# Attention pairs in one run of scores and one of values, small products in one place: a routed attention and mixer kernel on Trainium2

## The chip, the cores and the metric

The kernel runs on one core of one Trainium2 chip. A core has engines that work side by side, each through its own stream of instructions in order: TensorE (matrix products, called PE in the profile, with its weight loads under PEld), VectorE (DVE), ScalarE (ACT), GpSimd (POOL) and SyncE (SP), which issues transfers here. They wait for each other through semaphores. Matrix products are written to PSUM, a memory of eight banks; everything else lies in SBUF. The metric is the device time of the whole kernel in microseconds (us).

## What is computed

A routed attention with 4 batches and 8 heads, 768 tokens and head size 64, and after it an MLP mixer over tokens and channels:

```python
q_assign = argmax(einsum('bhsd,hcd->bhsc', q_n, c_n), axis=-1)     # 16 centroids per head
k_assign = argmax(einsum('bhsd,hcd->bhsc', k_n, c_n), axis=-1)
mask = q_assign[:, :, :, None] == k_assign[:, :, None, :]
scores = scale * matmul(q, k.transpose(0, 1, 3, 2))
scores = where(mask, scores, -1e9)
attn = softmax(scores)
attn_out = matmul(attn, v)
x = attn_out as (B, S, H * D)
h = maximum(x^T @ w_tok1, 0) @ w_tok2
u = x + h^T
out = u + maximum(u @ w_ch1, 0) @ w_ch2
```

(q_n, k_n and c_n are normalised rows. All arrays are fp32.)

## The kernel before

The attention goes over 16 pairs of heads (4 batches times 4 pairs). In a pair, two heads of 64 rows share TensorE, so its matmuls use parts of the 128 x 128 array. A pair's queries are two halves of 384 (`qh`), its keys six tiles of 128 (`j`). The scores and the mask are products into one PSUM tile of two banks; ScalarE takes the exponential into SBUF; VectorE adds the six exponentials of a half up; TensorE multiplies them with the values.

PSUM before: one bank `ps_w`, one bank `ps_av`, and three tiles of two banks `ps_sc`. The pools of SBUF that matter:

```python
    ps_w = pool("ps_w", 1, space=PSUM)
    ps_av = pool("ps_av", 1, space=PSUM)
    ps_sc = pool("ps_sc", 3, ps_sc_stack, space=PSUM)
    ...
    loads = pool("loads", 3, attention)      # values of a pair
    work = pool("work", 6, attention)        # exponentials
    sums = pool("sums", 2, attention)
    qkpool = pool("qkpool", 2, routing, side="right")
```

The products of a pair:

```python
    def scores(g, qh):
        ...
        for j in range(NJ):
            ...
            sc = ps_sc.tile([P, 2, 512], F32, tag="sc", name="sc")
            for src, start in ((st["ohT"], True), (st["T"], False)):
                for h in range(2):
                    rows = slice(h * D, (h + 1) * D)
                    nc.tensor.matmul(
                        sc[:, h, 0:HS], lhsT=src[rows, 1, j], rhs=src[rows, 0, js],
                        start=start, stop=not start,
                    )
            ex = st["ex", j] = work.tile([P, 2, HS], F32, name="ex")
            nc.scalar.activation(out=ex, in_=sc[:, :, 0:HS], func=ACT.Exp, scale=SM_SCALE)

    def add_up(g, qh):
        ...
        for j in range(1, NJ):
            nc.vector.tensor_tensor(
                out=acc, in0=acc if j > 1 else st["ex", 0], in1=st["ex", j], op=ALU.add
            )

    def values(g, qh):
        av = ps_av.tile([P, HS], F32, name="av")
        for j in range(NJ):
            ex = st.pop(("ex", j))
            for h in range(2):
                nc.tensor.matmul(
                    av[h * D : (h + 1) * D], lhsT=st["va"][:, h, j], rhs=ex[:, h],
                    start=(j == 0), stop=(j == NJ - 1),
                )
        ...
        nc.scalar.copy(out=st["avT"][:, js].rearrange("p j t -> p (j t)"), in_=av)
```

Beside these, each pair needs small products. `pair_sums` adds the sums up over the partitions (four column strips of 32, 384 wide), `route_products` multiplies the rows of a coming pair with the centroids (the same shape), `half_turn` transposes a half of the attention's result on TensorE (three transposes). What they give is taken by VectorE: `pair_denominators` and `pair_reciprocals`, `route` (a transpose, a maximum, two comparisons into one-hots), and `half_out`, which scales the result into the mixer's input. `turn` transposes the 32 x 32 blocks of a coming pair's queries and keys on VectorE, two instructions of 128 x 768. `route_turn` transposes one-hots through the DMA; `route_count` is a small sum on ScalarE.

The weights of the mixer are rounded during the attention. The work stands in 21 steps. One step does the VectorE and GpSimd part of piece i-2 (three VectorE instructions and one GpSimd add), the ScalarE part of piece i-1 (two instructions), and the load of piece i.

The loop before:

```python
    for g in range(NPAIR):
        more, old, final = g < NPAIR - 1, g - 1, g == NPAIR - 1
        if g + 2 < NPAIR:
            load(g + 2)
        ...
        scores(g, 0)
        if g == 0:
            turn(1)
        add_up(g, 0)
        rounding(1)
        values(g, 0)
        if more or old >= 0:
            two = ps_sc.tile([P, 2, 512], F32, tag="sc", name="small")
            if old >= 0:
                pair_sums(old, two[:, 0, 0:HS])
            if more:
                route_products(g + 1, two[:, 1, 0:HS])
            if old >= 0:
                pair_denominators(old)
            if more:
                route(g + 1)
                route_big(g + 1)
                route_turn(g + 1)
            if old >= 0:
                pair_reciprocals(old)

        scores(g, 1)
        if more:
            route_count(g + 1)
        add_up(g, 1)
        if g + 2 < NPAIR:
            turn(g + 2)
        values(g, 1)
        if old >= 0:
            two = ps_sc.tile([P, 2, 512], F32, tag="sc", name="px")
            for qh in range(2):
                half_turn(old, qh, two[:, qh, 0:HS])
            for qh in range(2):
                half_out(old, qh)
        rounding(g < EARLY or final)        # EARLY = 6
```

After the loop come the sums of the last pair in `ps_w`, then the mixer (token products `tok1` and `tok2`, then channel products), whose matmuls use the whole array.

Of the kernel before, what the change touches and what calls it, by code (L numbers as in the profile page):

```python
# [17 lines left out]
C = 16  # L18
P = 128
# [11 lines left out]
QP = P // NQ  # L31
NPAIR = B * NF

EARLY = 6
SM_SCALE = 0.125


# [8 lines left out]
def kernel(  # L46
# [37 lines left out]
            tc.tile_pool(name=name, bufs=bufs, reuse_waits="tile", **kw)  # L84
        )

    ps_w = pool("ps_w", 1, space=PSUM)
    ps_av = pool("ps_av", 1, space=PSUM)
    ps_sc_stack = fast.enter_context(ExitStack())
    ps_sc = pool("ps_sc", 3, ps_sc_stack, space=PSUM)  # L90

# [38 lines left out]
    def load(g):  # L130


        b, f = divmod(g, NF)
        st = state.setdefault(g, {})
        st["qk"] = qkpool.tile([P, 2, NJ, NQ, QP], F32, name="qk")
        st["va"] = loads.tile([P, 2, NJ, D], F32, name="va")
        for a, src in ((1, k), (0, q)):
            for c in range(NQ):
                h, d0 = 2 * f + c // 2, (c % 2) * QP
                nc.sync.dma_start(  # L140
                    st["qk"][c * QP : (c + 1) * QP, a].rearrange("r j i d -> r (j i) d"),
                    src[b, h, :, d0 : d0 + QP].rearrange("(i r j) d -> r j i d", i=NQ, j=NJ),
                )
        nc.sync.dma_start(
            st["va"], v[b, 2 * f : 2 * f + 2].rearrange("h (p j) d -> p h j d", p=P)
        )
# [91 lines left out]
    def centroids_norm(cen):  # L238
        sq = rsmall.tile([P, D], F32, name="censq")
        ss = rsmall.tile([P, 1], F32, name="ss")  # L240
        nc.vector.tensor_tensor(out=sq, in0=cen, in1=cen, op=ALU.mult)
        nc.vector.reduce_sum(out=ss, in_=sq, axis=AX.X)
        lo = rsmall.tile([P, 1], F32, name="lo")
        nc.vector.tensor_scalar_max(out=lo, in0=ss, scalar1=float(2.0**-100))


        nrm = rsmall.tile([P, 1], F32, name="nrm0")
        nc.vector.tensor_scalar(
            out=nrm.bitcast(I32), in0=lo.bitcast(I32), scalar1=0.5, scalar2=float(0x1FBB6875),
            op0=ALU.mult, op1=ALU.add,  # L250
        )
# [18 lines left out]
        pc = ps_w.tile([P, H * C], F32, tag="w", name="pc")  # L270
        nc.tensor.transpose(out=pc, in_=cn.rearrange("p i d -> p (i d)"), identity=ident)
        return pc

# [72 lines left out]


    def load_first():
        st = state[0] = {"qk": qkpool.tile([P, 2, NJ, NQ, QP], F32, name="qk")}
        st["va"] = loads.tile([P, 2, NJ, D], F32, name="va")  # L350
        st["T"] = qktp.tile([P, 2, NJ, P], F32, name="qkT")
        st["ohT"] = qktp.tile([P, 2, NJ, P], BF16, name="ohT")
        st["rows"] = st.pop("qk").rearrange("p a j i d -> p (a j i d)").rearrange(
            "p (n a j h d) -> p n a j h d", n=2, a=2, h=2, j=HJ
        )
        for n in range(2):
            for a, src, queue in ((1, k, nc.sync), (0, q, nc.scalar)):
                for h in range(2):
                    queue.dma_start(
                        st["rows"][:, n, a, :, h],  # L360
                        src[0, h].rearrange("(p j) d -> p j d", p=P)[:, HJ * n : HJ * n + HJ],
                    )
        nc.sync.dma_start(st["va"], v[0, 0:2].rearrange("h (p j) d -> p h j d", p=P))

    def turn_first(n, tiles):

        st = state[0]
        js = slice(HJ * n, HJ * n + HJ)
        for a in (1, 0):
            for j in range(HJ):  # L370
                nc.tensor.transpose(
                    out=tiles[a][:, j * P : (j + 1) * P],
                    in_=st["rows"][:, n, a, j].rearrange("p h d -> p (h d)"), identity=ident,
                )
        return [(st["T"][:, a, js].rearrange("p j t -> p (j t)"), tiles[a]) for a in range(2)]

    def route_turn_first(n):
        po = ps_w.tile([P, 2, HJ, P], BF16, tag="w", name="po")
# [27 lines left out]
    def scores(g, qh):  # L406
        st = state[g]
        js = slice(HJ * qh, HJ * qh + HJ)
        for j in range(NJ):
# [3 lines left out]
            for src, start in ((st["ohT"], True), (st["T"], False)):  # L413
                for h in range(2):
# [6 lines left out]
            nc.scalar.activation(out=ex, in_=sc[:, :, 0:HS], func=ACT.Exp, scale=SM_SCALE)  # L421

    def add_up(g, qh):
        st = state[g]
        if qh == 0:
            st["sum"] = sums.tile([P, 2, 2, HS], F32, name="sum")
        acc = st["sum"][:, qh]
        for j in range(1, NJ):
            nc.vector.tensor_tensor(  # L429
                out=acc, in0=acc if j > 1 else st["ex", 0], in1=st["ex", j], op=ALU.add  # L430
            )

    def values(g, qh):
        st = state[g]
        av = ps_av.tile([P, HS], F32, name="av")
        for j in range(NJ):
            ex = st.pop(("ex", j))
            for h in range(2):
                nc.tensor.matmul(  # L439
                    av[h * D : (h + 1) * D], lhsT=st["va"][:, h, j], rhs=ex[:, h],  # L440
# [285 lines left out]
            nc.vector.tensor_reduce(out=good[:, i : i + 1], in_=ok, axis=AX.X, op=ALU.min)  # L726

    def fits_count():
        pn = ps_w.tile([1, 3], F32, tag="w", name="pn")
# [11 lines left out]
    def begin():  # L741
# [11 lines left out]
        for oh in ohs:  # L753
            nc.gpsimd.memset(oh, 0.0)
        load(1)
        pw = ps_av.tile([P, HS], F32, name="av")

        def keep_warm(n):
            for _ in range(n):
# [29 lines left out]
    for b in range(B):  # L789
        if b + 1 < B:  # L790
            ends += [lambda b=b, t=t: tok1(b + 1, t) for t in range(NT)]
        ends += [lambda b=b, j=j: tok2(b, j) for j in range(NJ)]

    def rounding(n):
        for _ in range(min(n, len(weights))):
            weights.pop(0)()

    for g in range(NPAIR):
        more, old, final = g < NPAIR - 1, g - 1, g == NPAIR - 1
        if g + 2 < NPAIR:  # L800
            load(g + 2)
        if final:
            assert not weights
            routing.close()
            W["ch2"] = pool("wc2pool", 1, side="right").tile([P, NCT, DM], F32, name="wc2")
            weights = list(weight_steps(stage, W, ("ch2",)))

        scores(g, 0)
        if g == 0:
            turn(1)  # L810
        add_up(g, 0)
        rounding(1)
        values(g, 0)
        if more or old >= 0:
            two = ps_sc.tile([P, 2, 512], F32, tag="sc", name="small")
            if old >= 0:
                pair_sums(old, two[:, 0, 0:HS])
            if more:
                route_products(g + 1, two[:, 1, 0:HS])
            if old >= 0:  # L820
                pair_denominators(old)
            if more:
                route(g + 1)
                route_big(g + 1)
                route_turn(g + 1)
            if old >= 0:
                pair_reciprocals(old)

        scores(g, 1)
        if more:  # L830
            route_count(g + 1)
        add_up(g, 1)
        if g + 2 < NPAIR:
            turn(g + 2)
        values(g, 1)
        if old >= 0:
            two = ps_sc.tile([P, 2, 512], F32, tag="sc", name="px")
            for qh in range(2):
                half_turn(old, qh, two[:, qh, 0:HS])
            for qh in range(2):  # L840
                half_out(old, qh)
        rounding(g < EARLY or final)

    pair_sums(NPAIR - 1, ps_w.tile([P, HS], F32, tag="w", name="den"))
    pair_denominators(NPAIR - 1)
    pair_reciprocals(NPAIR - 1)
    ps_sc_stack.close()
    pools["ps_m"] = pool("ps_m", 2, space=PSUM)
    for m in range(9):
        ends.pop(0)()  # L850
        if m == 0:
            half_turn(NPAIR - 1, 0, ps_w.tile([P, HS], F32, tag="w", name="px"))
            half_turn(NPAIR - 1, 1, ps_av.tile([P, HS], F32, name="av"))
            for qh in range(2):
                half_out(NPAIR - 1, qh)
        if m % 3 == 2:
# [243 lines left out]
```

## Time and profile before

| | |
|---|---|
| time, median of 3 | 877.78 us (877.59 to 877.98) |
| span of the profiled execution | 875.5 us |
| TensorE busy | 862.4 us, 4294 matmuls |
| VectorE busy | 504.9 us |
| ScalarE busy | 297.8 us |
| GpSimd busy | 44.2 us |
| granted TensorE clock | 0.998 |

The attention takes the first 333 us of the span, the mixer the rest. A line of the profile's groups gives the source line, the engine and the operation, then what it writes and reads with shapes. For a matmul the shape begins with the part of the array that it uses, rows * columns: 64*128 is one of two row halves, 128*64 one of two column halves, 128*32 one of four strips. An fp32 product stands as two matmuls. A matmul's recorded length covers its way through the array, and neighbours overlap, so what one costs in a stream is read from the distance of starts and not from its length. In a timeline, neighbours of one kind are merged; the first number is the start, the second how long the merged run lasts, and a bracket tells the idle time before it and who ended it.

### The profile page before, as it was taken

Reading aid. Unit: us, or ns where it says so; the run is one execution under the profiler, and the core shown is the slowest. Engines: PE = TensorE matmul, PEld = TensorE weight load, DVE = VectorE, ACT = ScalarE, POOL = GpSimd, SP = SyncE. Lnnn points to the kernel's source line nnn. Section 1 sums busy time; section 2 is a strip of 40 time slices with the busy share of each in tenths; the row PEclk is TensorE's granted clock in tenths of the full one; section 3 lists DMA queues with packets and bytes.
Section 4 is the critical chain, followed back from the end, with each engine's and each line's share of the span. In section 5 each row is a group of like instructions: output and inputs, shape, how many; then the busy total and the mean of one; then the engine's idle time right before and its main releaser. Section 6 shows DMA issues by size and latency. Waiting matters only on the chain.

```text
span 875.5 us, 11022 instructions
## 1 busy us (share of the span) xinstructions
PE 862.4 (99%) x4294; PEld 522.8 (60%) x4294; DVE 504.9 (58%) x848; ACT 297.8 (34%) x506; POOL 44.2 (5%) x40
## 2 busy tenths in 40 slices
PE   9999999999999999999999999999999999999996
PEld 4444444444444444444578686685876867768675
DVE  6798898888878862895553433423344333443332
ACT  4666566666556551321210211203112031130210
POOL 1010011000010000330000000000000000000000
PEclk9999999999999999999999999999999999999999
DMA  8665675544443130420000010000010000100001
GB/s 153 156 123 119 140 139 115 126 109 97 97 97 73 20 90 0 144 72 1 0 1 1 0 37 37 0 1 0 36 38 1 0 1 25 48 1 1 0 25 51
DMA packets 133275, 47.61 MB, mean 54 GB/s; under 512 B 122080, under 2 KB 126176, under 8 KB 133216
## 3 DMA queue, kind: packets, MB, share of 16 engines
q1 hardware_dynamic: 131616, 46.45, 23.0%
q8 instruction: 35, 0.57, 0.3%
q10 hardware_dynamic: 1600, 0.39, 0.2%
q14 instruction: 24, 0.20, 0.1%
HBM read 34.64 MB, written 6.29 MB: 47 GB/s over the span
## 4 chain that ended last, share of the span: by engine, by line
PE 95%; DVE 3%; ACT 1%; issue 0%; DVEq 0%
PE sc L416 18%; PE av L439 15%; PE pX L690 14%; PE pX L639 14%; PE pZ L690 7%; PE pZ L639 7%; PE ph L508 4%; PE pY L690 4%; PE pY L639 4%; PE pu L517 3%; PE px L468 1%; PE small L455 1%; PE pt L580 1%; PE small L296 1%; DVE wh L209 1%; DVE wT L214 1%
## 5 line engine op out<-in xcount | busy, mean ns | idle before, releaser
L421 ACT ACTIVATE ex<-sc 128x768 f32<-128x768 f32 x192 | 152.6, 811 | 44.8 <-PE sc L416 42.6
L416 PE MATMUL sc<-qkT 64*128 64x384 f32 x768 | 155.1, 482 | 0.0
L429 DVE TENSOR_TENSOR sum<-sum,ex 128x768 f32<-128x768 f32 x128 | 125.3, 979 | 13.7 <-ACT ex L421 0.5
L439 PE MATMUL av<-ex,va 128*64 128x384 f32 x768 | 130.9, 490 | 0.0
L439 PEld LDWEIGHTS av<-ex,va 128*64 128x64 f32 x768 | 52.2, 137 | 74.8 <-issue 71.0
L416 PEld LDWEIGHTS sc<-qkT 64*128 64x128 f32 x768 | 68.2, 188 | 34.8 <-issue 34.6
L639 PE MATMUL pX<-uT,wc 128*128 128x384 f32 x192 | 67.4, 487 | 0.0
L416 PE MATMUL sc<-ohT 64*128 64x384 bf16 x384 | 63.0, 324 | 0.3 <-DVE ohT L389 0.2
L647 ACT COPY p<-pX 128x384 f32<-128x384 f32 x24 | 11.4, 475 | 148.1 <-PE pX L639 148.1
L639 PEld LDWEIGHTS pX<-uT,wc 128*128 128x128 f32 x192 | 36.2, 190 | 24.7 <-issue 1.0
L221 POOL TENSOR_TENSOR wc<-wT,wup 128x512 int32<-128x512 int32 x24 | 32.0, 1334 | 253.5 <-ACT avT L446 132.0
L429 DVE TENSOR_TENSOR sum<-ex 128x768 f32<-128x768 f32 x32 | 32.0, 1001 | 20.3 <-ACT ex L421 20.2
L446 ACT COPY avT<-av 128x384 f32<-128x384 f32 x32 | 15.3, 479 | 83.1 <-PE av L439 83.1
L508 PE MATMUL ph<-x,wt 128*128 128x512 f32 x96 | 42.0, 594 | 1.2 <-DVE x L520 0.7
L517 PE MATMUL pu<-h,wt 128*128 128x512 f32 x96 | 42.0, 592 | 0.0
L534 DVE TENSOR_TENSOR c<-pZ,u 128x384 f32<-128x384 f32 x24 | 13.4, 557 | 46.9 <-PE pZ L639 46.9
L416 PEld LDWEIGHTS <-ohT 64*128 64x128 bf16 x384 | 19.2, 94 | 35.4 <-issue 13.6
L534 DVE TENSOR_TENSOR x<-pX,x 128x256 f32<-128x256 f32 x24 | 10.2, 423 | 49.3 <-PE pX L690 49.3
L534 DVE TENSOR_TENSOR hA<-pY,p 128x384 f32<-128x384 f32 x24 | 13.4, 557 | 40.4 <-PE pY L639 40.4
L690 PE MATMUL pX<-w2s,hA 128*128 128x256 f32 x144 | 35.1, 380 | 0.5 <-DVE x L534 0.5
L690 PE MATMUL pX<-wc,hA 128*128 128x256 f32 x144 | 35.0, 379 | 0.0
L690 PE MATMUL pZ<-w2s,hS 128*128 128x256 f32 x144 | 35.0, 379 | 0.0
(129 smaller groups left out, 1196.5 us busy)
## 6 DMA issues: line engine op xcount, KB each, us to landing
raw<-in_moe_w_ch_dram SPq DMA_DIRECT2D x24, 512.0 KB, 4.3
qk<-in_k_dram SPq DMA_DIRECT2D x64, 96.0 KB, 4.0
va<-in_v_dram SPq DMA_DIRECT2D x16, 384.0 KB, 4.0
out_dram<-x SPq DMA_DIRECT2D x24, 256.0 KB, 2.0
qk<-in_q_dram SPq DMA_DIRECT2D x60, 96.0 KB, 3.4
raw<-in_moe_w_tok_dram SPq DMA_DIRECT2D x3, 512.0 KB, 4.6
raw<-in_moe_w_tok_dram SPq DMA_DIRECT2D x4, 384.0 KB, 4.0
qk<-in_q_dram ACTq DMA_DIRECT2D x4, 96.0 KB, 3.1
```

The costliest lines, as they stand in the source:

```text
L221: nc.gpsimd.tensor_tensor(out=dst.bitcast(I32), in0=T, in1=up, op=ALU.add)
L416: nc.tensor.matmul(sc[:, h, 0:HS], lhsT=src[rows, 1, j], rhs=src[rows, 0, js], start=start, stop=not start,)
L421: nc.scalar.activation(out=ex, in_=sc[:, :, 0:HS], func=ACT.Exp, scale=SM_SCALE)
L429: nc.vector.tensor_tensor(out=acc, in0=acc if j > 1 else st["ex", 0], in1=st["ex", j], op=ALU.add)
L439: nc.tensor.matmul(av[h * D : (h + 1) * D], lhsT=st["va"][:, h, j], rhs=ex[:, h], start=(j == 0), stop=(j == NJ - 1),)
L446: nc.scalar.copy(out=st["avT"][:, js].rearrange("p j t -> p (j t)"), in_=av)
L508: nc.tensor.matmul(pf, lhsT=W["tok1"][:, j, t * P : (t + 1) * P], rhs=xs[b][:, j], start=(j == 0), stop=(j == NJ - 1),)
L517: nc.tensor.matmul(pu, lhsT=W["tok2"][:, t, j], rhs=h1s[b][:, t], start=(t == 0), stop=(t == NT - 1))
L534: nc.vector.tensor_tensor(out=dst, in0=a, in1=b, op=ALU.add)
L639: nc.tensor.matmul(psum, lhsT=A[a][:, k, c * P : (c + 1) * P], rhs=R[r][:, k], start=start and k == 0, stop=k == 1, skip_group_check=not s ...
L647: nc.scalar.copy(out=kept[name], in_=psum)
L690: nc.tensor.matmul(psum, lhsT=h2[a][:, k, i * P : (i + 1) * P], rhs=Bw[w][:, 3 * part + k], start=start and k == 0, stop=k == 2, skip_grou ...
```

## The change

A pair is treated as one unit. Both halves' scores come first, all 12 blocks, then both halves' values. The small products come at one place per pair: the transposes of the pair before, then the sums of this pair and the route products of the pair after next in one PSUM tile. So the routing runs two pairs ahead instead of one. For 12 blocks of exponentials there are nine buffers, and the three score tiles in PSUM hold the rest. `ps_w` goes, and `ps_av` has two banks, so that the second half's values needn't wait for the copy of the first. A rounding step stands between scores and values in each pair, and six of the pairs have a second one at their end; before, the first six pairs had a second one after the values. Loads of values are issued on their own, and the rows of the first pair are loaded into two of the exponential buffers.

The aim of the order is that TensorE stays longer with one kind of product. The diff, with small renamings cut (`...`):

```diff
-EARLY = 6
+EARLY = 13
+
+EX = 9
...
-    ps_w = pool("ps_w", 1, space=PSUM)
-    ps_av = pool("ps_av", 1, space=PSUM)
+    ps_av = pool("ps_av", 2, space=PSUM)
...
-    loads = pool("loads", 3, attention)
+    loads = pool("loads", 2, attention)
...
-    work = pool("work", 6, attention)
+    work = pool("work", EX, attention)
...
-            ex = st["ex", j] = work.tile([P, 2, HS], F32, name="ex")
+            ex = st["ex", qh, j] = work.tile([P, 2, HS], F32, name="ex")
...
-            st["sum"] = sums.tile([P, 2, 2, HS], F32, name="sum")
+            st["sum"] = sums.tile([P, 2, 2, HS], F32, name="sum", bufs=1)
...
+    load_v(1)
     for g in range(NPAIR):
-        more, old, final = g < NPAIR - 1, g - 1, g == NPAIR - 1
-        if g + 2 < NPAIR:
-            load(g + 2)
+        final = g == NPAIR - 1
...
-        (the loop's body as shown above)
+        for qh in range(2):
+            scores(g, qh)
+            if g == 0 and qh == 0:
+                turn(1)
+                load(2)
+            if (g, qh) == (0, 1):
+                route_products(1, ps_av.tile([P, HS], F32, tag="av", name="pr"))
+                route_on(1)
+            add_up(g, qh)
+        for other in (1, 2) if g == 1 else (g + 1,) if 2 <= g < NPAIR - 1 else ():
+            route_count(other)
         if g + 2 < NPAIR:
             turn(g + 2)
+        if g + 3 < NPAIR:
+            load(g + 3)
+        rounding(1)
+        for qh in range(2):
+            values(g, qh)
+        if g + 2 < NPAIR:
+            load_v(g + 2)
+
+        if g > 0:
             two = ps_sc.tile([P, 2, 512], F32, tag="sc", name="px")
             for qh in range(2):
+                half_turn(g - 1, qh, two[:, qh, 0:HS])
+        two = ps_sc.tile([P, 2, 512], F32, tag="sc", name="small")
+        pair_sums(g, two[:, 0, 0:HS])
+        if g + 2 < NPAIR:
+            route_products(g + 2, two[:, 1, 0:HS])
+        if g > 0:
+            for qh in range(2):
+                half_out(g - 1, qh)
+        pair_denominators(g)
+        if g + 2 < NPAIR:
+            route_on(g + 2)
+        pair_reciprocals(g)
+        rounding(final or g % 2 == 0 and 0 < g < EARLY)
+
-    pair_sums(NPAIR - 1, ps_w.tile([P, HS], F32, tag="w", name="den"))
-    pair_denominators(NPAIR - 1)
-    pair_reciprocals(NPAIR - 1)
...
```

(`route_on` is `route`, `route_big` and `route_turn` in one.)

More of the change, by code (lines that the diff above doesn't have):

```diff
@@ L135, in load @@
         st["qk"] = qkpool.tile([P, 2, NJ, NQ, QP], F32, name="qk")
-        st["va"] = loads.tile([P, 2, NJ, D], F32, name="va")
         for a, src in ((1, k), (0, q)):
@@ L143, in load, with load_v @@
                 )
+    def load_v(g):
+        b, f = divmod(g, NF)
+        st = state[g]
+        st["va"] = loads.tile([P, 2, NJ, D], F32, name="va")
         nc.sync.dma_start(
@@ L269, in centroids_norm @@
         )
-        pc = ps_w.tile([P, H * C], F32, tag="w", name="pc")
+        pc = ps_av.tile([P, H * C], F32, tag="av", name="pc")
         nc.tensor.transpose(out=pc, in_=cn.rearrange("p i d -> p (i d)"), identity=ident)
@@ L348, in load_first @@
     def load_first():
-        st = state[0] = {"qk": qkpool.tile([P, 2, NJ, NQ, QP], F32, name="qk")}
-        st["va"] = loads.tile([P, 2, NJ, D], F32, name="va")
+        st = state[0] = {}
         st["T"] = qktp.tile([P, 2, NJ, P], F32, name="qkT")
         st["ohT"] = qktp.tile([P, 2, NJ, P], BF16, name="ohT")
-        st["rows"] = st.pop("qk").rearrange("p a j i d -> p (a j i d)").rearrange(
-            "p (n a j h d) -> p n a j h d", n=2, a=2, h=2, j=HJ
-        )
+        st["rows"] = [
+            work.tile([P, 2, HS], F32, name="ex").rearrange("p a (j h d) -> p a j h d", h=2, d=D)
+            for _ in range(2)
+        ]
         for n in range(2):
@@ L359, in load_first @@
                     queue.dma_start(
-                        st["rows"][:, n, a, :, h],
+                        st["rows"][n][:, a, :, h],
                         src[0, h].rearrange("(p j) d -> p j d", p=P)[:, HJ * n : HJ * n + HJ],
                     )
-        nc.sync.dma_start(st["va"], v[0, 0:2].rearrange("h (p j) d -> p h j d", p=P))
     def turn_first(n, tiles):
@@ L372, in turn_first @@
                     out=tiles[a][:, j * P : (j + 1) * P],
-                    in_=st["rows"][:, n, a, j].rearrange("p h d -> p (h d)"), identity=ident,
+                    in_=st["rows"][n][:, a, j].rearrange("p h d -> p (h d)"), identity=ident,
                 )
@@ L377, in route_turn_first @@
     def route_turn_first(n):
-        po = ps_w.tile([P, 2, HJ, P], BF16, tag="w", name="po")
+        po = ps_av.tile([P, 2, HJ, P], BF16, tag="av", name="po")
         for a in (1, 0):
@@ L429, in add_up @@
             nc.vector.tensor_tensor(
-                out=acc, in0=acc if j > 1 else st["ex", 0], in1=st["ex", j], op=ALU.add
+                out=acc, in0=acc if j > 1 else st["ex", qh, 0], in1=st["ex", qh, j], op=ALU.add
             )
@@ L434, in values @@
         st = state[g]
-        av = ps_av.tile([P, HS], F32, name="av")
+        av = ps_av.tile([P, HS], F32, tag="av", name="av")
         for j in range(NJ):
-            ex = st.pop(("ex", j))
+            ex = st.pop(("ex", qh, j))
             for h in range(2):
@@ L728, in fits_count @@
     def fits_count():
-        pn = ps_w.tile([1, 3], F32, tag="w", name="pn")
+        pn = ps_av.tile([1, 3], F32, tag="av", name="pn")
         nc.tensor.matmul(pn, lhsT=ones[:, 0:1], rhs=good, start=True, stop=True)
@@ L755, in begin @@
         load(1)
-        pw = ps_av.tile([P, HS], F32, name="av")
+        load_v(0)
+        pw = ps_av.tile([P, HS], F32, tag="av", name="av")
         def keep_warm(n):
@@ L792, with route_on @@
         ends += [lambda b=b, j=j: tok2(b, j) for j in range(NJ)]
+    def route_on(g):
+        route(g)
+        route_big(g)
+        route_turn(g)
     def rounding(n):
@@ L806 @@
             weights = list(weight_steps(stage, W, ("ch2",)))
[L808 to L832, printed above, removed]
+        for qh in range(2):
[9 more added lines that the diff above has]
+            route_count(other)
@@ L833 @@
         if g + 2 < NPAIR:
             turn(g + 2)
-        values(g, 1)
-        if old >= 0:
+        if g + 3 < NPAIR:
[6 more added lines that the diff above has]
+        if g > 0:
             two = ps_sc.tile([P, 2, 512], F32, tag="sc", name="px")
             for qh in range(2):
-                half_turn(old, qh, two[:, qh, 0:HS])
-            for qh in range(2):
-                half_out(old, qh)
@@ L842 @@
-        rounding(g < EARLY or final)
-    pair_sums(NPAIR - 1, ps_w.tile([P, HS], F32, tag="w", name="den"))
-    pair_denominators(NPAIR - 1)
-    pair_reciprocals(NPAIR - 1)
+                half_turn(g - 1, qh, two[:, qh, 0:HS])
[4 more added lines that the diff above has]
+        if g > 0:
+            for qh in range(2):
+                half_out(g - 1, qh)
@@ L851 @@
         if m == 0:
-            half_turn(NPAIR - 1, 0, ps_w.tile([P, HS], F32, tag="w", name="px"))
-            half_turn(NPAIR - 1, 1, ps_av.tile([P, HS], F32, name="av"))
+            half_turn(NPAIR - 1, 0, ps_av.tile([P, HS], F32, tag="av", name="px"))
+            half_turn(NPAIR - 1, 1, ps_av.tile([P, HS], F32, tag="av", name="av"))
             for qh in range(2):
```

## The prediction

> **What bounds the kernel now.** I read the busy table first, then the chain, then TensorE's timeline over one pair of heads, then the other engines over the same stretch. The first two, from the page of the kernel before:
>
> ```profile
> PE 862.4 (99%) x4294; PEld 522.8 (60%) x4294; DVE 504.9 (58%) x848; ACT 297.8 (34%) x506; POOL 44.2 (5%) x40
> ...
> PE 95%; DVE 3%; ACT 1%; issue 0%; DVEq 0%
> ```
>
> TensorE never rests. No other engine's wait can be shortened to any use; the time falls only if TensorE does less, or does the same with fewer losses between matmuls. The waits of TensorE that the trace names come to about 7 us in the whole run, with none in the 15 full pairs. So I looked at one pair on TensorE, instruction by instruction (columns: start, length, instruction; lines of the score loop left out):
>
> ```profile
> 251.71 0.34 PE L416 MATMUL sc<-ohT 64*128 64x384 bf16 x2
> ...
> 255.76 0.33 PE L416 MATMUL sc<-ohT 64*128 64x384 bf16 x2
> 255.92 0.81 PE L416 MATMUL sc<-qkT 64*128 64x384 f32 x4
> 256.66 4.09 PE L439 MATMUL av<-ex,va 128*64 128x384 f32 x24
> 260.68 0.85 PE L455 MATMUL small<-sum,ones 128*32 128x384 f32 x8
> 261.35 0.83 PE L296 MATMUL small<-qkT,cnd 128*32 128x384 f32 x8
> 262.11 0.34 PE L416 MATMUL sc<-ohT 64*128 64x384 bf16 x2
> ...
> 271.08 0.88 PE L468 MATMUL px<-ident,avT 128*128 128x128 f32 x6
> 271.89 0.34 PE L416 MATMUL sc<-ohT 64*128 64x384 bf16 x2
> ```
>
> The pair takes 271.89 - 251.71 = 20.18 us. In it TensorE changes its tile shape six times: 64*128 (scores) to 128*64 (values) to 128*32 (small) to 64*128 to 128*64 to 128*128 (px) to 64*128. Within one shape the starts in the trace are evenly spaced: a score block of one key tile 0.807, a step of two value matmuls 0.3225, a step of four small ones 0.322, a px transpose 0.109. At a change of shape the last step is longer, in every one of the 15 pairs alike: 0.416 after scores, 0.422 after values, 0.439 after small (by starts of the step's first matmul; 0.322 each without a change), 0.205 after px for 0.109. The first step of the new shape is a little longer too: 0.374 for the first value step, 0.346 for small, 0.169 for px, and 0.011 more for scores. Together a change costs:
>
> - scores to values 0.094 + 0.051 = 0.145
> - values to small 0.100 + 0.023 = 0.123; values to px 0.100 + 0.060 = 0.160
> - small to scores 0.117 + 0.011 = 0.128; px to scores 0.096 + 0.011 = 0.107
>
> Check: work without changes is 12 x 0.807 + 24 x 0.3225 + 4 x 0.322 + 6 x 0.109 = 19.37; changes 0.145 x 2 + 0.123 + 0.128 + 0.160 + 0.107 = 0.81; sum 20.18, as measured. In the mixer part after the pairs, where all is 128*128, going from one kind of product to another shows no such step (0.429 before and at the border). The loss belongs to the shape.
>
> **What the Trainium skill says.** "TensorEngine Tiling (Array Packing)", Tiling Modes, Key Properties: "Changing tiling mode (not just tile) drains the TensorE". The trace agrees, about 0.10 us a time. "TensorE: Matmul & The Clock Gate", Part 2, Step-by-step, says that between matmuls of a stream the drain of one overlaps the fill of the next; agreed, a pair of 384-column bf16 matmuls is 0.162 apart from what follows. "GPSIMD Engine Reference", 1. Specifications, says GpSimd shares SBUF interfaces with VectorE and contends with an instruction that has two SBUF inputs. The adds are such: four take 4.15 us alone, 5.03 beside a rounding add of GpSimd.
>
> **The change, part by part.**
>
> *Order on TensorE.* The pair becomes 12 score blocks, 12 value blocks, px of the pair before, then sums and route products as one run of 128*32. Four changes of shape: scores to values 0.145, values to px 0.160, px to small, small to scores 0.128. Px to small is seen once before, at the end of the attention (px at 330.97, sums at 331.78: 0.81, as px to scores): 0.096 + 0.023 = 0.12. Sum 0.55 for 0.81: **0.255 us less per pair**, period 19.92. The count of matmuls is the same. Fifteen pairs: 3.8 us.
>
> *Last pair.* Its sums come with the other small ones and no longer as a group of their own: the same count of changes is saved, already counted in the 3.8; I add 0.1 for the extra change that the old end had.
>
> *First pair.* Sums of pair 0 and products for pair 2 now stand at its end. The products need pair 2's transposed rows, and VectorE turns those after adding up pair 0. Scores begin at 10.14, go on to about 20.5, products for pair 1 to 21.3, values to 29.3, sums to 30.0. VectorE: route of pair 1 from 21.4 (2.1 us), five adds 5.15 to 28.7, turn 1.8 to 30.5. So TensorE waits there about 0.5 us, once.
>
> *Exponentials: nine buffers and three score tiles in PSUM for 12 blocks.* Blocks 10 to 12 are computed into PSUM, but their exponentials wait until the first value blocks give buffers back. Times from the first score matmul of a pair: values start at 9.8, the first block is through at 10.6, exponential 10 runs to 11.5, 11 and 12 follow at 0.72 (the spacing that ScalarE showed when it was behind) to 12.9. TensorE needs exponential 10 only in the tenth value block, at 9.8 + 9 x 0.645 = 15.6. No wait.
>
> *VectorE.* A pair's busy time is 16.3 us with one rounding step and 18.6 with two; both under 19.9. But the order counts now:
>
> ```profile
> 254.45 0.96 DVE L429 TENSOR_TENSOR sum<-ex 128x768 f32<-128x768 f32 x1 [1.61 <-ACT ex L421]
> 255.51 4.15 DVE L429 TENSOR_TENSOR sum<-sum,ex 128x768 f32<-128x768 f32 x4
> 259.58 0.42 DVE L204 TENSOR_SCALAR wh<-wh 128x512 f32<-128x512 f32 x1
> ...
> 262.24 0.58 DVE L459 STREAM_TRANSPOSE dent<-small 128x384 f32<-128x384 f32 x1 [0.99 <-PE small L296]
> ...
> 264.85 0.96 DVE L429 TENSOR_TENSOR sum<-ex 128x768 f32<-128x768 f32 x1
> ```
>
> From these: adds begin 2.74 after the pair (254.45 - 251.71), five take 5.13, rounding 1.6, the block from denominators to reciprocals 2.6. In the new order: seven adds to 9.95, three more behind the late exponentials 11.6 to 14.7, turn to 16.4, rounding to 18.0. The last px transpose starts at 18.3 and half_out can follow 0.3 later (as 271.68 to 271.99 before): 18.6 to 19.6, denominators and the route transpose to 20.7, the rest to 22.2. TensorE wants px's tile back for the second score block at 20.7 and the small tile for the third at 21.5: 1.1 and 0.8 us of slack. The next adds start at 19.92 + 2.74 = 22.7, after 22.2. With a second rounding step, at the end of six pairs, VectorE reaches the next adds 1.15 late and loses 0.9 to GpSimd, most of which its wait for exponential 10 takes up: the add that would start at 11.6 starts at about 12. Still in time for half_out.
>
> *Buffers and loads.* Rows, values and one-hots are asked for about a pair ahead of use or more; a load takes 4 us. Off the path. The larger exponential pool replaces the third load buffer and the second sum buffer; the sum tile is read at 18.5 and written again 4 us later.
>
> Sum: 15 x 0.255 + 0.1 (end) + 0.1 (one change fewer in pair 0) - 0.5 (wait in pair 0) = 3.5 us. 877.8 - 3.5 = **874.2**.
>
> **Rivals.**
> 1. *The exponentials become a gate.* If a buffer came back only when the whole first half of the values is done, exponential 10 would start near 13.9: adds to 18, turn to 20, route products (wanted at 19.1) late by over 1, half_out with rounding near 22.5, the second score block late by 2. Some 2 to 2.5 us a pair, 30 to 38 us in all, near 910. Against it: today a reader's release is seen one matmul group after it (exponential 1 starts at 252.74, 0.53 after its last score matmul starts), and the buffer's readers are two value matmul pairs.
> 2. *VectorE's order bites in the pairs with two roundings.* My slack there is under 1 us. If it is used up in six to twelve pairs by 0.3 to 0.5 us, 2 to 5 us are lost: 876 to 879. For it: adds of up to 1.84 us beside GpSimd in the trace. Against it: the step that collided with the adds is at most once per place now.
> 3. *The drain isn't saved.* If px to small cost much more than the single sight at 331.78 says, or the border between the two score halves or the two value halves cost something, 0.1 to 0.2 a pair goes: 876.
>
> **Range and chances.** All terms are under half a per cent. Without stalls 873.7; rival 2 or 3 in part, 876 to 877. I take 873.0 to 877.0. Over 2% faster isn't in reach, since no TensorE work goes; over 2% slower needs rival 1.
>
> **What would show it.** Right: TensorE at 99% again with no waits in the pairs, pair period 19.9, the first sums of pair 1 directly before a score run, exponentials 10 to 12 spaced by the value blocks, first mixer product near 329.4 (333.06 before). Wrong: TensorE waits on half_out, the route transpose or turns in each pair, or VectorE without a wait before its adds.

## The result and the profile after

The changed kernel takes **873.8 us** (median of 6, 873.6 to 874.59) for 877.8 us of the kernel before (median of 6). The ratio is 0.9956, with a 95% interval of 0.9943 to 0.9968: 2.8 to 5.0 us are gone. Predicted were 874.2 us, 873.0 to 877.0.

The same two lines of the page, busy times and chain:

```profile
PE 858.7 (99%) x4294; PEld 525.3 (60%) x4294; DVE 502.8 (58%) x848; ACT 296.6 (34%) x506; POOL 45.7 (5%) x40
...
PE 94%; DVE 4%; ACT 1%; issue 0%; DVEq 0%
```

As many matmuls as before, TensorE as full as before, and its busy time is 3.7 us shorter. A busy time that falls with the count unchanged says that the matmuls stand closer together. TensorE's timeline over one pair shows where (score loop left out):

```profile
211.08 0.34 PE L420 MATMUL sc<-ohT 64*128 64x384 bf16 x2
...
220.87 7.96 PE L443 MATMUL av<-ex,va 128*64 128x384 f32 x48
228.76 0.88 PE L472 MATMUL px<-ident,avT 128*128 128x128 f32 x6
229.57 0.85 PE L459 MATMUL small<-sum,ones 128*32 128x384 f32 x8
230.24 0.83 PE L301 MATMUL small<-qkT,cnd 128*32 128x384 f32 x8
231.00 0.34 PE L420 MATMUL sc<-ohT 64*128 64x384 bf16 x2
```

The 48 value matmuls are one run, where two of 24 stood before. The pair takes 231.00 - 211.08 = 19.92 us, and no line has a wait. From pair 1 to pair 13 every pair takes 19.92 by the starts in the trace, with one rounding step or two.

The exponentials and VectorE in the same pair (ScalarE's lines first, then VectorE's):

```profile
212.11 7.27 ACT L425 ACTIVATE ex<-sc 128x768 f32<-128x768 f32 x9 [2.67 <-PE sc L420]
221.78 2.22 ACT L425 ACTIVATE ex<-sc 128x768 f32<-128x768 f32 x3 [2.40 <-PE av L443]
```

```profile
222.63 3.08 DVE L433 TENSOR_TENSOR sum<-sum,ex 128x768 f32<-128x768 f32 x3 [1.73 <-ACT ex L425]
225.63 1.83 DVE L291 STREAM_TRANSPOSE qkT<-qk 128x768 f32<-128x768 f32 x2
...
229.68 1.02 DVE L480 TENSOR_TENSOR x<-px,rcps 128x384 f32<-128x384 f32 x2 [0.65 <-PE px L472]
231.13 0.58 DVE L463 STREAM_TRANSPOSE dent<-small 128x384 f32<-128x384 f32 x1 [0.44 <-PE small L301]
```

The tenth exponential waits 2.40 us for the first value blocks, the last three adds wait 1.73 us for it, and then VectorE is still early: it waits 0.65 us for px and 0.44 us for the small products. So the new waits exist, and they lie on engines that have time. This is a pair that does not follow a second rounding step. Of the six that do, five (pairs 3, 7, 9, 11 and 13) have less room: VectorE does not wait for px there, and half_out begins at 18.68 after the pair's start, in pair 7 at 19.02, for 18.60 here. TensorE waits for nothing in these pairs either.

### The profile page after: what moved, and what is told of

It reads as the page before. It is cut to its first block, busy times and chain, and to the rows that moved or that the text cites. A ratio compares the mean times of both kernels' runs of the same rounds, so it can differ in the third digit from the quotient of the medians.

```text
span 871.6 us, 11036 instructions
## 1 busy us (share of the span) xinstructions
PE 858.7 (99%) x4294; PEld 525.3 (60%) x4294; DVE 502.8 (58%) x848; ACT 296.6 (34%) x506; POOL 45.7 (5%) x40
## 4 chain that ended last, share of the span: by engine, by line
PE 94%; DVE 4%; ACT 1%; issue 0%; DVEq 0%
PE sc L420 18%; PE pX L694 14%; PE pX L643 14%; PE av L443 14%; PE pZ L694 7%; PE pZ L643 7%; PE ph L512 4%; PE pY L694 4%; PE pY L643 4%; PE pu L521 3%; PE px L472 1%; PE small L459 1%; PE pt L584 1%; PE small L301 1%; DVE wh L214 1%; DVE wT L219 1%
## 5 line engine op out<-in xcount | busy, mean ns | idle before, releaser
L433 DVE TENSOR_TENSOR sum<-sum,ex 128x768 f32<-128x768 f32 x128 | 127.7, 997 | 28.3 <-ACT ex L425 15.6
L443 PE MATMUL av<-ex,va 128*64 128x384 f32 x768 | 127.4, 488 | 0.0
L694 PE MATMUL pY<-wc,hA 128*128 128x256 f32 x144 | 35.0, 379 | 0.0
L694 PE MATMUL pX<-w2s,hS 128*128 128x256 f32 x144 | 35.0, 379 | 0.0
```

The source lines that it names most:

```text
L433: nc.vector.tensor_tensor(out=acc, in0=acc if j > 1 else st["ex", qh, 0], in1=st["ex", qh, j], op=ALU.add)
L443: nc.tensor.matmul(av[h * D : (h + 1) * D], lhsT=st["va"][:, h, j], rhs=ex[:, h], start=(j == 0), stop=(j == NJ - 1),)
L694: nc.tensor.matmul(psum, lhsT=h2[a][:, k, i * P : (i + 1) * P], rhs=Bw[w][:, 3 * part + k], start=start and k == 0, stop=k == 2, skip_grou ...
```

## The experiments

Twelve kernels follow, all of them edits of the changed kernel; in the diffs `...` stands for what is left out. Ratios are to the kernel before, with 95% intervals; the changed kernel stands at 0.9956. A pair's length is taken from the start of its first score matmul to that of the next pair's.

### Back to the halves, small products still in one place

```diff
             add_up(g, qh)
+            if g > 0 and qh == 0:
+                rounding(1)
+                values(g, 0)
...
-        rounding(1)
-        for qh in range(2):
-            values(g, qh)
+        if g == 0:
+            rounding(1)
+            values(g, 0)
+        values(g, 1)
```

> From pair 1 on the order of the halves before the change (scores, values, scores, values), with the rounding step again between the first half's adds and values; the small products stay at one place after px, nine buffers stay. Theory (each change of tile shape costs TensorE its own part): two more changes per pair, scores to values 0.145 and values to scores about 0.113, so 0.258 x 15 = 3.9 us: 877.7, pair period 20.18; bringing the small products together is then worth nothing by itself. Rival (the gain comes from having small products at one place): stays near 873.8 to 875.5.

Measured: 880.24 us, ratio 1.0026 (1.0015 to 1.0038). By starts, nine of the fourteen pairs from 1 to 14 take 20.18 us (the last of them less its route products), which is the theory's number and also that of the kernel before, whose small products stand in two places. So having them in one place is worth nothing by itself; the gain comes with the two changes of shape that the long runs of scores and values save. But five pairs, each behind one that ended with a second rounding step, took 20.5 to 21.0, some 2.3 us more in all, which the expectation had not foreseen. At the end of one of them TensorE's line of route products shows the visible part of it:

```profile
171.97 0.85 PE L459 MATMUL small<-sum,ones 128*32 128x384 f32 x8
173.11 0.85 PE L301 MATMUL small<-qkT,cnd 128*32 128x384 f32 x8 [0.29 <-DVE qkT L291]
```

VectorE was late with the transposes of rows. In this pair the second half's adds start late, after a wait of 0.48 us for an exponential; ScalarE itself was late there, because its part of the rounding step had waited 3.46 us for VectorE. And one of these adds ran beside a GpSimd add (1.75 us where it takes 0.95 else). That is rival 2 of the prediction, in an order in which VectorE has less room.

### Two shape changes put back

```diff
+        if g > 0:
+            two = ps_sc.tile([P, 2, 512], F32, tag="sc", name="px")
         for qh in range(2):
             values(g, qh)
+            if g > 0:
+                half_turn(g - 1, qh, two[:, qh, 0:HS])
...
-        (px after both values)
```

> The changed kernel with px in two halves, three transposes after each half of the values, and nothing else moved: sc av px av px small. Theory: one more values to px (0.160) and px to values (about 0.096 + 0.051 = 0.147) per pair, 0.307 x 15 = 4.6 us: 878.4, period 20.23. Rival (the gain came from VectorE or ScalarE waiting less): half_out can even start earlier, 873.8.

Measured: 878.2 us, ratio 1.0003 (0.9995 to 1.0012). The pair takes 20.22 for 20.23 expected. Nothing but the place of three transposes differs from the changed kernel, and the whole gain is gone. The three in the middle, with a change before and behind them, begin 0.48 us before the next values, for 3 x 0.109 = 0.33 without a change:

```profile
227.30 0.55 PE L472 MATMUL px<-ident,avT 128*128 128x128 f32 x3
227.78 4.09 PE L443 MATMUL av<-ex,va 128*64 128x384 f32 x24
```

### Ten shape changes put back

```diff
+            if between is not None and j % 2 == 1:
+                nc.tensor.transpose(
+                    out=between[:, (j // 2) * P : (j // 2) * P + P],
+                    in_=state[g - 1]["avT"][:, HJ * qh + j // 2], identity=ident,
+                )
...
```

> The dose: the six px transposes one by one, each after two value blocks, so five more pairs of changes than the changed kernel and not one. Theory: 5 x 0.307 = 1.54 us per pair, 15 pairs 23.0 us: 896.8, and a straight line through the changed kernel, px_split and this one. If a change cost a fixed drain only where the run before it is long, this lies clearly below the line.

Measured: 901.04 us, ratio 1.0264 (1.0249 to 1.028): 4.2 us over the line. The list of waits has the rest (columns: us in total, times, longest):

```profile
PE px L448 <- ACT ex L425: 4.0, 15, 0.3
```

The first transpose comes only two value blocks into the run, and px's tile is that of exponential 10, which isn't done by then. Without these 4.0 us it is 897.0 for 896.8 expected. The dose is a straight line: pairs of 19.92, 20.22 and 21.76 - 0.27 = 21.49 us with 0, 1 and 5 more changes there and back, 0.30 and 0.31 us each. A change costs the same after a run of two value blocks as after one of six or twelve.

### The control: another kind of product, the same shape

```diff
+                if (i + n) % 2 == 0:
+                    nc.tensor.matmul(st["den"][rows], lhsT=ones, rhs=acc[:, :, rows], ...)
+                else:
+                    nc.tensor.matmul(other["pr"][rows], lhsT=cnd[...], rhs=other["T"][...], ...)
```

> The control: the sums and the route products of a pair alternate matmul by matmul (strips 0 and 2 of one, 1 and 3 of the other, then the rest), so the kind changes seven times and not once, and the tile shape 128*32 never. Theory (the loss belongs to the shape): 873.8 within 0.5. Rival (the loss comes with a new kind of product, its operands or its PSUM bank): six more changes of about 0.1 in 14 pairs, 8 us more, 882.

Measured: 874.24 us, ratio 0.9962 (0.9949 to 0.9976). Pairs take 19.92 again, and the small products take 1.43 us to the next scores, as in the changed kernel (231.00 - 229.57):

```profile
229.93 0.51 PE L812 MATMUL small<-sum,ones 128*32 128x384 f32 x1
229.94 0.51 PE L816 MATMUL small<-qkT,cnd 128*32 128x384 f32 x1
...
231.36 0.34 PE L420 MATMUL sc<-ohT 64*128 64x384 bf16 x2
```

The 0.4 us lie in pair 0, whose length rises from 18.96 to 19.60 (start of the first long score run to the next pair), because half of the sums now waits with the products for the transposed rows.

The control is weaker than it was meant to be. In the order that was run the kind changes six times, not seven, and the four strips work side by side (their starts are 0.007 apart), so that each strip changes its kind just once, as in the changed kernel. A stronger control stands in every score block of every kernel here. There the kind changes within one shape, from the fp32 product of one block to the bf16 product of the next with its own PSUM tile, and the last fp32 step takes 0.323 us, the same as any other; before the values, where the shape changes, it takes 0.416. So the loss belongs to the tile shape.

### Both rounding steps in one place

```diff
-        rounding(1)
+        rounding(1 + (not final and g % 2 == 0 and 0 < g < EARLY))
...
-        rounding(final or g % 2 == 0 and 0 < g < EARLY)
+        rounding(final)
```

> The changed kernel with the second rounding step of six pairs put beside the first, between scores and values. Theory (VectorE has about 0.8 us before TensorE waits on px's and the small tile): the step takes 1.6 us plus a wait of about 0.4 on the GpSimd add before it, half_out ends near 21.0 and the route transpose near 22.1 after the pair's start for 20.7 and 21.5 wanted, 0.3 to 0.6 us lost in each of six pairs: 875.5 to 877.5, with TensorE waiting in those pairs. Rival (VectorE's total of 18.6 us in a 19.9 us pair is what counts): 873.8.

Measured: 877.57 us, ratio 0.9998 (0.9989 to 1.0006), 3.8 us more than the changed kernel and just above the range expected. One such pair on VectorE, then GpSimd, then TensorE:

```profile
231.15 0.42 DVE L209 TENSOR_SCALAR wh<-wh 128x512 f32<-128x512 f32 x1
231.60 1.38 DVE L214 TENSOR_SCALAR wh<-wh 128x512 uint32<-128x512 uint32 x1
233.08 0.69 DVE L219 SCALAR_TENSOR_TENSOR wT<-raw,wh 128x512 uint32<-128x512 uint32 x1
233.69 1.01 DVE L480 TENSOR_TENSOR x<-px,rcps 128x384 f32<-128x384 f32 x2
```

```profile
231.37 1.32 POOL L226 TENSOR_TENSOR wc<-wT,wup 128x512 int32<-128x512 int32 x1 [18.66 <-DVE wT L219]
```

```profile
233.20 0.34 PE L420 MATMUL sc<-ohT 64*128 64x384 bf16 x2
233.38 0.81 PE L420 MATMUL sc<-qkT 64*128 64x384 f32 x4
234.76 0.34 PE L420 MATMUL sc<-ohT 64*128 64x384 bf16 x2 [0.57 <-DVE x L480]
```

The second score block waits for half_out to give px's tile back. Its start should follow 0.81 after the first and follows 1.56 after; four pairs lose 0.8 to 0.9, one 0.4, one 0.1. So placing the second step at the pair's end is worth all that the change gains: the same work in the same pair, 3.8 us apart.

What is lost is not the step's own length alone. Its middle instruction (L214) runs beside the GpSimd add of the step before and takes 1.38 us, for 0.43 in the first step. These 0.95 us are more than the 0.75 by which the second score block is late. The same instruction is slowed in all six pairs, by 0.95 in the four that lose most and by 0.7 in the other two. As an estimate from these lines, without the slowdown half_out would have ended near 233.75, before the 234.01 at which the second score block was due; no run here has the second step there without the GpSimd add beside it.

### The late exponential, two attempts

The first attempt took the value blocks in the order 1, 2, 3, 4, 5, 0:

```diff
-        for j in range(NJ):
+        order = [*range(1, NJ), 0] if qh == 0 else [*range(NJ)]
+        for j in order:
...
```

> The changed kernel, but the values of the first half take the exponentials in the order 1, 2, 3, 4, 5, 0, so that the buffer for exponential 10 comes back only at the end of that half, 3.2 us later. No work and no change of shape is added. Theory (VectorE's last adds follow exponential 10 and half_out, turn and rounding follow them): route products late by 0.5, second score block by 0.9, third by 0.3, some 1.7 us in each pair with rounding: 20 to 25 us more, 894 to 899, period 21.6. Rival (TensorE is the bound and the other engines have two us of slack a pair): 873.8 to 875.

Measured: 873.52 us, ratio 0.9948 (0.9933 to 0.9963). That decides nothing: exponential 10 starts at 222.16, 0.92 after the values (221.24), and in the changed kernel it is 0.91 as well. So it can't have waited for the buffer that this order reads last, and the delay was never made. The second attempt makes it on ScalarE:

```diff
...
+            if 0 < g < NPAIR - 1 and (qh, j) == (1, HJ):
+                for _ in range(27):
+                    nc.scalar.copy(out=scratch, in_=ident)
             ex = st["ex", qh, j] = work.tile([P, 2, HS], F32, name="ex")
```

> The changed kernel with 27 small copies of no use (128 x 128) on ScalarE between exponentials 9 and 10 of pairs 1 to 14, where ScalarE has 2.4 us to spare, so that exponentials 10 to 12 start about 3 us later (near 13.9 after the pair's start for 10.7). It is the price of rival 1 by itself; no work of TensorE and no change of shape is added. Theory (VectorE's last adds, turn, rounding and half_out follow the exponentials one behind the other, with under 1 us of slack at the end): products, second and third score block late by some 1.7 us in pairs with rounding: 20 to 25 us more, 894 to 899. Rival (two us of slack per pair on VectorE in total take it up): 873.8 to 876.

Measured: 938.47 us, ratio 1.069 (1.0673 to 1.0706). The dose was twice what was meant: the copies took 0.33 us each, where I had reckoned 0.2. ScalarE, then TensorE:

```profile
235.44 8.86 ACT L427 COPY scratch<-ident 128x128 f32<-128x128 f32 x27
244.20 2.21 ACT L429 ACTIVATE ex<-sc 128x768 f32<-128x768 f32 x3
```

```profile
245.06 2.27 PE L447 MATMUL av<-ex,va 128*64 128x384 f32 x12 [2.04 <-ACT ex L429]
...
249.92 0.85 PE L302 MATMUL small<-qkT,cnd 128*32 128x384 f32 x8 [0.81 <-DVE qkT L292]
...
252.41 0.34 PE L421 MATMUL sc<-ohT 64*128 64x384 bf16 x2 [0.72 <-DVE x L484]
```

The copies exceed ScalarE's 2.4 idle us by 6.5. The kernel is 64.7 us longer than the changed one, 4.6 for each of the 14 pairs. Not all of it is waiting: in six of these pairs (1, 2, 3, 8, 11 and 12) TensorE's granted clock fell to 0.50 for 3.41 us behind the wait for the exponential, and a value step took 0.63 us there for 0.32. That is at most 1.7 us each and 10 us in all. So of the 6.5 us some 2 to 2.6 were taken up and the rest was paid, through the waits that the prediction named for rival 1 (products on the turn, second score block on half_out) and through one that it didn't, the value blocks themselves. The size expected was for another dose and isn't confirmed.

### Eleven buffers for nine

```diff
-EX = 9
+EX = 11
...
-            st["avT"] = sums.tile([P, NJ, P], F32, name="avT")
+            b, f = divmod(g, NF)
+            st["avT"] = xs[b][:, :, f * P : (f + 1) * P]
```

> Eleven buffers of exponentials for nine; the space comes from keeping the attention's result before px in the mixer's input tile, where it ends anyway. Theory (nine buffers and three score tiles in PSUM are enough, TensorE waits for none): exponentials 10 and 11 no longer wait and VectorE is done sooner, time 873.8 within 0.5. Rival (the nine buffers hold TensorE back somewhere): faster by 1 us or more.

Measured: 873.69 us, ratio 0.9952 (0.9938 to 0.9965), pairs of 19.92. In the pair at 212 us eleven exponentials now run without a break and only the twelfth waits (0.79 us), and nothing is gained. Nine are enough: the wait for a buffer is off the path.

### The wait in pair 0

```diff
...
             if (g, qh) == (0, 1):
+                turn(2, (1,))
                 route_products(1, ...)
...
-            turn(g + 2)
+            turn(g + 2, (0,) if g == 0 else (1, 0))
```

> Takes away the one wait inside the attention: in pair 0 the transpose of pair 2's keys on VectorE is put before the route of pair 1, in a stretch where VectorE idles, so that only the queries are turned after the adds. Theory: the 0.47 us wait of the route products goes: 873.3, first scores of pair 1 0.47 us sooner. If route of pair 1 comes too late for it, nothing or a loss.

Measured: 873.4 us, ratio 0.9945 (0.9932 to 0.9959). Pair 0 is 0.37 us shorter (18.59 for 18.96, from its first long score run), somewhat less than the 0.47 expected: the named wait is gone, but the products still start 0.89 after the sums and not 0.67. The interval alone wouldn't separate it from the changed kernel; the trace does.

### Fewer changes than in the changed kernel

```diff
-        if g > 0:
+        old = [o for o in (g - 2, g - 1) if o >= 0] if g % 2 else []
+        for o in old:
             two = ps_sc.tile([P, 2, 512], F32, tag="sc", name="px")
             for qh in range(2):
-                half_turn(g - 1, qh, two[:, qh, 0:HS])
+                half_turn(o, qh, two[:, qh, 0:HS])
...
```

> Fewer changes of shape than in the changed kernel: px of two pairs together in every odd pair (those without a second rounding), none in the even ones; the attention's result waits in the mixer's input tile. In a pair without px, values to small 0.123 replaces values to px 0.160 and px to small 0.12: 0.157 less, in 7 pairs: 1.1 us, 872.7. The odd pairs bear two more half_outs (1.0 us) on VectorE: if px's or the small tile is then given back late there, 0.2 to 0.5 us is lost in each of 8 pairs and the gain is gone: 873 to 876.

Measured: 872.74 us, ratio 0.9941 (0.9928 to 0.9955). Pairs take 20.575 and 19.115 in turn by starts: 39.69 for two, 0.15 under two of 19.92. The longer ones are 19.92 and six transposes of 0.109, so VectorE's two more half_outs cost nothing.

Then px of half of the pairs was moved into the mixer:

```diff
+        old = (g - 3, g - 2) if g in (3, 5, 7, 9) else ()
...
-        if m == 0:
+        for o in (8 + m,) if m < 8 else ():
+            for qh in range(2):
+                half_turn(o, qh, ps_av.tile([P, HS], F32, tag="av", name="px"))
```

> Goes on from px_pairs and turn_early: px of pairs 0 to 7 by twos in four pairs, px of pairs 8 to 15 one after another between the first token products of the mixer, where the tile shape is 128*128 anyway. Theory: eleven pairs without px save 11 x 0.157 = 1.7 us, the early turn 0.4: 871.7. If VectorE, which takes 8.5 us of half_out over into the mixer, becomes the bound there, the gain is smaller or gone: 872.5 to 876.

Measured: 874.87 us (873.13 to 875.77), ratio 0.9958 (0.9944 to 0.9972). A loss against px_pairs, and the second case is why:

```profile
357.70 1.01 PE L474 MATMUL px<-ident,x 128*128 128x128 f32 x6 [2.14 <-DVE x L482]
358.55 5.29 PE L523 MATMUL pu<-h,wt 128*128 128x512 f32 x8
```

The eight matmuls behind the wait take 5.29 us, for 3.60 in the changed kernel: the granted clock was 0.50 for 3.41 us there. By the starts the wait costs 2.3 us and the lower clock 1.7. Of the five times two lie at 873.1 and 873.5, with a mean clock of 0.998 for the whole run, and three at 874.9 to 875.8, with 0.996; a fall of the clock in these three alone would make that difference, but only one of them has a trace. From the fifth product on, a mixer product takes 1.7 us and VectorE has an add, two half_outs and every third time two rounding steps for it. The early ones cost nothing: there a product takes 5.2 us. So the last kernel keeps only those:

```diff
-        old = (g - 3, g - 2) if g in (3, 5, 7, 9) else ()
+        old = (g - 3, g - 2) if 1 < g < 14 and g % 2 else ()
...
-        for o in (8 + m,) if m < 8 else ():
+        for o in (12 + m,) if m < 4 else ():
```

> What px_late and px_pairs showed put together: px of pairs 0 to 11 by twos in six odd pairs (3 to 13), px of pairs 12 to 15 between the first four token products of the mixer only, where VectorE idles over 4 us at a time in px_late, and the early turn of turn_early. Nine pairs without px save 9 x 0.157 = 1.4 us, the early turn 0.4: 872.0 from 873.8, with no wait for half_out in the mixer. If VectorE is late there even so, 873 to 875.

Measured: **871.88 us** (871.57 to 872.57), ratio 0.9932 (0.9919 to 0.9946), less than the kernel before and the changed kernel. The steps in the mixer run without a wait, and six transposes take 331.71 - 331.06 = 0.65 us there, 6 x 0.109, with no change to pay:

```profile
331.06 0.82 PE L474 MATMUL px<-ident,x 128*128 128x128 f32 x6
331.71 5.32 PE L514 MATMUL ph<-x,wt 128*128 128x512 f32 x12
```

## Why the prediction was right, step by step

**Changes of shape.** Right in kind and size. The period was reckoned 19.92 and is 19.92. The one new border, px to small, takes 0.202 for 0.109 at its exit in all 15 pairs, as the single sight before had promised. Putting two changes back (px_split) takes the gain away, ten (px_six) lie on the same line, and a change of kind without shape (mixed_kinds and every score block) costs nothing. That TensorE drains at such a change is what the Trainium skill says ("TensorEngine Tiling (Array Packing)", Tiling Modes, Key Properties); the runs show only that the time goes with the shape.

**VectorE's order.** Exponential 10 was put at 10.6 after the pair's start and stands at 10.7 (221.78 - 211.08), the late adds at 11.6 and stand at 11.55, half_out at 18.6 and stands at 18.60. The slack was real, but not all of it was sized rightly. At px's tile it is the 1.1 us stated in most pairs (half_out ends at 19.62, the second score block is due at 20.73) and 0.69 in pair 7; in the five pairs with less room the late adds start at 12.4 or later, for the 12 expected. At the small tile it is 0.43 in every full pair, for 0.8 stated: the route transpose ends at 21.1 and not at 20.7, since VectorE has to wait for the route products (the 0.44 above). Nothing was lost to it, but rival 2 was nearer than the prediction had it: round_two, with its slowdown beside GpSimd, goes beyond it and loses 3.8 us.

**The wait of pair 0.** Reckoned 0.5. TensorE's timeline has it:

```profile
31.01 0.85 PE L301 MATMUL small<-qkT,cnd 128*32 128x384 f32 x8 [0.47 <-DVE qkT L291]
```

By the starts it is 0.65 (31.01 - 29.69 = 1.32 for 0.67).

**The ends of the sum.** From the first score to the first mixer product it is 4.3 us less, for 3.5 in the sum. Two waits of the kernel before were missing from it: one of 0.42 for half_out at the mixer's start, which its timeline shows, and one of 0.27 in pair 0, seen only in starts (a score block at 22.33 that follows 1.07 after its predecessor for 0.81). Both are gone in the changed kernel; the runs don't show why (at the mixer's start the same matmuls stand in the same order in both). The mixer begins at 329.31. The prediction had said 329.4, though its own sum gives 333.06 - 3.5 = 329.6:

```profile
329.31 5.42 PE L512 MATMUL ph<-x,wt 128*128 128x512 f32 x12
```

So that this place agrees to 0.1 us is in part luck: most of the missing 0.8 is made up for by the scores, which in this profile begin 0.54 later than before (10.68 for 10.14), with two of the warm-up matmuls of no use taking 0.84 for 0.49. In the other kernels with the same beginning the first score starts between 10.3 and 11.2; whether the new beginning is later as such, or only scatters, one profile of the kernel before can't tell.

**A reading.** The waits that the trace of the kernel before names for TensorE add up to 5.1 us, and not to about 7 as the prediction has it. Nothing in its sum rests on this.

**The rivals.** Rival 1 didn't occur: the release of a buffer is seen 0.9 us into the values. That late exponentials would be paid for is shown by late_exp; the 2 to 2.5 us a pair that I gave for it were not tested at that dose. Rival 2 isn't in the changed kernel, but in its neighbours halves and round_two, in both with an instruction of VectorE slowed beside a GpSimd add. Rival 3 is out: the borders inside the scores and inside the values cost nothing, as the period shows.

## What to carry to other kernels

Where TensorE is full, read the starts of its matmuls, not their lengths: count the borders between tile shapes, take the extra step at each, and order the products so that there are fewer of them. A longer run of one kind moves every other engine's work into bunches, so before trusting the gain, follow the engine that gives the tiles back through one pair by time, not by its total, and look at what runs beside it. Transposes that use the whole array are free of the change where the products around them use the whole array too, as long as the engine that takes them away has room there.

## What the hardware showed that was not expected

A rounding instruction of VectorE with one input (line 214) took 1.38 us beside a GpSimd add and 0.43 alone; I had looked for such a loss only in the adds with two inputs (0.95 alone, 1.75 beside GpSimd in the halves kernel). 27 copies of 128 x 128 on ScalarE, one after another into the same tile, took 0.33 us each (8.86 in all), where 0.2 had been reckoned. And a wait of TensorE can cost more than its length: behind 7 of the 15 waits of about 2 us in the traces of late_exp (14) and px_late (1) the granted clock was 0.50 for 3.41 us, and behind the other eight it stayed at 1.00. What decides between the two is not shown.
